# Packed rows kept block behind block and stored eight at a time, a weight fetched as one element, and smaller load slots, in a kernel that reads its input in one pass and writes it scaled in a second

## The chip, the cores and the metric

The kernel runs on one core of one Trainium2 chip. The metric is the device time of one execution in microseconds (us); the time before is the median of three runs. The core has a matrix engine (PE, with its weight loads PEld), a vector engine (DVE), a scalar engine (ACT), GpSimd (POOL) and a sync engine (SP). In this kernel SP does nothing but issue loads, and ACT issues the stores besides its own work. Loads and stores all run on the core's 16 DMA engines.

## The reference

```python
H = W = C = 384                      # x: 1 x H x W x C, bfloat16; w1d: one element
g = jnp.einsum("bhwc->bc", x) / (H * W)
s = jax.nn.sigmoid(g * w1d[0])       # the window k is 1, so nothing is padded
return x * s[:, None, None, :]
```

Each of the 384 channels is averaged over all 147,456 positions. The average, times one weight and through a sigmoid, scales that channel. No output can be written before all of the input has been read, and the input (113.25 MB) is larger than the memory on the core.

## The kernel before

The positions are cut into 1152 "rows". A row of the kernel is one position for each of the 128 partitions, 384 bf16 values each: 768 bytes per partition, 98,304 bytes together. All rows pass through one tile, `arena`, of 275 rows; a range of rows in it is reused for one chunk of the input after another.

**First pass.** SP issues loads in program order. PE sums every row that lands (`sum_rows`, L215 to L239): a matmul with a matrix of ones adds the row into the accumulator `acc`, 1152 matmuls in all. A load into rows that are in use waits until PE has summed what was there. What can stay on the core isn't read again in the second pass:

- 18 rows are copied by ACT into the accumulator memory's seven other banks (`c_ps`, L316);
- 95 rows stay as they are in the parts A (47 rows), Y, U and T (16 each);
- 240 rows are folded. `QS = [16, 16, 16, 12]` gives four groups. In a group with `q`, three times `q` rows `w` stay in one of four areas, and the bits of `q` further rows `u` are hidden in their exponents. `fold` (L272) does that in 15 pieces of 4 `u` rows and 12 `w` rows, with T and Y as scratch rows, and ACT sums a check word for each piece into `seen` (L290), which says later whether any value was out of range.

The other 799 rows (`N_STREAM`) are read in the first pass for their sums alone, and once more in the second pass. The order of loads is written out by hand: `SLOTS` cuts A into load slots, `BEFORE[g]` lists what is streamed ahead of the rows `w` of group `g`, `BETWEEN[g]` what comes between its `w` and its `u`, and `AFTER` what comes behind the last group. At the end come the rows that stay in A, Y and U, and T in parts of 8, 4, 2, 1 and 1 rows (L364).

**The turn.** ACT forms the scale `s_bf` with a sigmoid from `acc` and `w_sc` (L370). `w_sc` is the weight over the number of positions, on all 128 partitions.

**Second pass.** DVE multiplies rows by `s_bf` in place (`scale`, L375), ACT issues their store (`store`, L385), and SP reloads the freed rows with the next of the 799. `unfold` (L393) restores a folded piece, scales it, and stores its 12 `w` rows (L424) and its 4 `u` rows. `from_psum` does the 18 rows of the banks. The order on DVE, ACT and SP comes from a small planner that runs while the program is built (L507 to L619). It keeps two modelled DMA queues, and at each step picks either the next landed rows to scale or, when over `IDLE` = 22 us of DMA work is queued, the next piece to unfold.

`Flow` (L21) turns all this into semaphore waits: each step names the rows that it reads and writes, and the waits follow from that. An area `w` is free for loads once all its pieces are stored.

Of the kernel before, what the change touches and what calls it, by code (L numbers as in the profile page):

```python
# [128 lines left out]
def kernel(  # L129
# [43 lines left out]
    w_bf = pool.tile([P, 1], bf16, name="w_bf")  # L173
# [51 lines left out]
    def sum_rows(a, n):  # L225
# [3 lines left out]
        for i in range(a, a + n):  # L229
            first, last = summed[0] == 0, summed[0] == RPP - 1  # L230
            fl.add(
                "PE", lambda i=i, f=first, l=last: emit(i, f, l),
                reads=[("a", i), "ones"], writes=["acc"],
            )
            summed[0] += 1

# [3 lines left out]

    def dve(fn, out, in_, reads, writes, **kw):
        fl.add("DVE", lambda: getattr(nc.vector, fn)(out=out, **in_, **kw), reads=reads, writes=writes)
# [22 lines left out]
    def three(a, p):  # L265
        return arena[:, a : a + 3 * p, :].rearrange("p (j q) c -> p j q c", j=3).bitcast(u16)

# [4 lines left out]
    def fold(k):  # L272
        g, lo, p = pieces[k]
        w, wc = area(g, lo, p)
        wall = wc[0] + wc[1] + wc[2]
        ua, ta, ya = RAW["U"][0] + lo, RAW["T"][0], RAW["Y"][0]
# [8 lines left out]
        join(w, w, three(ta, p), XOR, wall + rows(ta, 3 * p), wall)  # L285
        join(w[:, 2], w[:, 2], flat(ta + 3 * p, p), XOR, wc[2] + rows(ta + 3 * p, p), wc[2])
# [8 lines left out]
    fl.add("ACT", lambda: nc.scalar.dma_start(out=w_bf[:], in_=w1d.to_broadcast((P, 1))), writes=["w_bf"], dma=True)  # L295
    fl.add("DVE", lambda: nc.vector.memset(ones[:], 1.0), writes=["ones"])  # L296
    fl.add(
        "DVE",
        lambda: nc.vector.tensor_scalar_mul(out=w_sc[:], in0=w_bf[:], scalar1=1.0 / float(HW)),  # L299
        reads=["w_bf"], writes=["w_sc"],  # L300
# [8 lines left out]
    A, Y, U, T = (RAW[n][0] for n in "AYUT")  # L309
# [11 lines left out]
    def stream_all(where, n=None):  # L321
# [9 lines left out]
    SLOTS = [(A, 16), (A + 16, 16), (A + 32, 15)]  # L331
    BEFORE = [
        None,
        areas[2:4] + [(A, 12)],
# [3 lines left out]
    BETWEEN = [[], [], [(A, 13)], [(A, 16)]]  # L338
# [25 lines left out]
    for lo, hi in ((0, 8), (8, 12), (12, 14), (14, 15), (15, 16)):  # L364
# [6 lines left out]
        reads=["acc", "w_sc"], writes=["s_bf"],  # L371
# [21 lines left out]
    def unfold(k, half):  # L393

        g, lo, p = pieces[k]
        q = QS[g]
        w, wc = area(g, lo, p)
        wall = wc[0] + wc[1] + wc[2]
        ra, ba, ca = T + half * PIECE, T + 2 * PIECE, T + 3 * PIECE
        u, b, c = flat(ra, p), flat(ba, p), flat(ca, p)  # L400
        uc, bc, cc = rows(ra, p), rows(ba, p), rows(ca, p)
        bits(u, w[:, 0], SHR, 4, AND, 0x0780, wc[0], uc)
        bits(b, w[:, 1], SHR, 8, AND, 0x0078, wc[1], bc)
        bits(c, w[:, 2], SHR, 12, AND, 0x0007, wc[2], cc)
        join(u, u, b, OR, uc + bc, uc)
        bits(b, w[:, 2], SHL, 4, AND, 0x8000, wc[2], bc)
        join(u, u, c, OR, uc + cc, uc)
        bits(w, w, AND, 0x87FF, OR, 0x3800, wall, wall)
        join(u, u, b, OR, uc + bc, uc)
        wv = w.bitcast(bf16)  # L410
        fl.add(
            "DVE",
            lambda: nc.vector.tensor_tensor(  # L413
                out=wv, in0=wv, in1=s_bf[:, None, None, :].to_broadcast([P, 3, p, C]), op=Op.mult
            ),
# [237 lines left out]
```

## Time and profile before

| | us |
|---|---|
| median of 3 runs | 737.12 (735.68 to 737.66) |
| the profiled execution, its own time | 736.57 |
| its span, first to last instruction | 734.8 |
| DVE busy | 450.7 |
| PE busy | 208.1 |
| ACT busy | 86.7 |

The memory outside the core is read for 191.79 MB and written for 113.25 MB, at 415 GB/s over the span. The profile's page gives busy times in 40 slices of the span, the waits, and the instructions grouped by line and by shape. A line such as L247 is that of a helper (`bits`), so the shape tells which call it was: 128x1536 is four rows of 384, 128x4608 is twelve. A "window" view gives for each stretch of time the busy time of each engine, the clock granted to PE, the busy share of the 16 DMA engines, and the bytes they moved as GB/s. A DMA row with the suffix q is the issue by that engine's queue, not the transfer.

### The profile page before, as it was taken

To read this page: it belongs to the slowest core of one execution; us is meant where nothing else is said; L and a number is where in the kernel's file an instruction comes from. 1 tells how busy PE (TensorE), PEld (TensorE's weight loads), DVE (VectorE), ACT (ScalarE), POOL (GpSimd) and SP (SyncE) were. 2 spreads that over 40 slices of the span, in tenths; PEclk is the share of its full clock that TensorE was granted. 3 is DMA by queue.
4 is the path that set the end of the run, shared out by engine and by line. 5 is a ranking of instruction groups with operands and counts; after the bars stand their busy time and mean duration, and the time that the engine had idled before them with its cause. 6 is when DMAs were issued, how large, how long until landed. Compare 5 with 4: busy or idle time off the path is not lost.

```text
span 734.8 us, 3038 instructions
## 1 busy us (share of the span) xinstructions
PE 208.1 (28%) x1153; PEld 115.9 (16%) x1153; DVE 450.7 (61%) x399; ACT 86.7 (12%) x39; POOL 0.2 (0%) x4
## 2 busy tenths in 40 slices
PE   2877896968687770000000000000000000000000
PEld 1443453535344330000000000000000000000000
DVE  0000002969697709799997579969099999194600
ACT  2000000747475600000000000000000000000000
POOL 0000000000000000000000000000000000000000
PEclk9799998999899995555555555555555555555555
DMA  8999999999999979999999999999999999999996
GB/s 351 426 436 436 427 437 418 442 416 435 417 412 414 387 319 338 431 408 428 428 426 431 427 427 426 440 421 428 421 427 428 439 433 409 426 444 408 425 431 292
DMA packets 29775, 305.25 MB, mean 415 GB/s; under 512 B 3008, under 2 KB 3776, under 8 KB 12992
## 3 DMA queue, kind: packets, MB, share of 16 engines
q1 hardware_dynamic: 12096, 191.80, 61.9%
q10 hardware_dynamic: 17664, 113.25, 36.7%
q8 instruction: 9, 0.15, 0.1%
q14 instruction: 6, 0.05, 0.0%
HBM read 191.79 MB, written 113.25 MB: 415 GB/s over the span
## 4 chain that ended last, share of the span: by engine, by line
DMA 44%; DVE 37%; ACT 7%; PE 4%; ACTq 1%; issue 0%; SPq 0%; DVEq 0%
DMA arena<-in_x_dram 25%; DVE arena L379 19%; DMA out_dram<-arena 19%; DVE arena L247 10%; ACT arena L290 7%; DVE arena L253 4%; PE bank L227 4%; DVE arena L413 4%; ACTq L389 1%; SPq L221 0%; DVEq L106 0%; ACT s_bf L370 0%; PE bank L472 0%; DVE odd L467 0%; DVE odd_i L476 0%
## 5 line engine op out<-in xcount | busy, mean ns | idle before, releaser
L247 DVE TENSOR_SCALAR arena<-arena 128x1536 uint16<-128x1536 uint16 (+1 forms) x210 | 123.8, 639 | 192.3 <-DMA arena<-in_x_dram 126.1
L227 PE MATMUL bank<-arena,ones 128*128 128x384 bf16 x1152 | 207.9, 344 | 66.7 <-DMA arena<-in_x_dram 66.5
L379 DVE TENSOR_TENSOR arena<-arena,s_bf 128x6144 bf16<-128x6144 bf16 (+7 forms) x79 | 198.0, 2567 | 32.6 <-ACT s_bf L370 22.2
L227 PEld LDWEIGHTS bank<-arena,ones 128*128 128x128 bf16 x1152 | 115.8, 102 | 158.4 <-DMA arena<-in_x_dram 68.1
L290 ACT ACTIVATE arena<-arena 128x6144 uint16<-128x6144 uint16 x15 | 79.9, 5324 | 161.8 <-DVE arena L247 161.8
L253 DVE TENSOR_TENSOR arena<-arena 128x1536 uint16<-128x1536 uint16 (+1 forms) x75 | 95.3, 1270 | 1.7 <-PE bank L227 1.1
L413 DVE TENSOR_TENSOR arena<-arena,s_bf 128x4608 bf16<-128x4608 bf16 x15 | 38.3, 2550 | 0.0
L472 PE MATMUL bank<-odd,ones 128*128 128x1 bf16 x1 | 0.2, 186 | 39.7 <-DVE odd L467 39.7
L299 DVE TENSOR_SCALAR w_sc<-w_bf 128x1 f32<-128x1 bf16 x1 | 0.2, 154 | 13.4 <-DMA w_bf<-in_w1d_dram 13.4
L472 PEld LDWEIGHTS bank<-odd,ones 128*128 128x128 bf16 x1 | 0.1, 104 | 40.1 <-DVE odd L467 40.1
L451 DVE TENSOR_TENSOR arena<-bank,s_bf 128x768 bf16<-128x768 bf16 (+2 forms) x15 | 5.0, 390 | 0.1
L316 ACT COPY bank<-arena 128x512 uint32<-128x512 uint32 (+1 forms) x7 | 3.6, 565 | 6.4 <-DMA arena<-in_x_dram 6.4
L370 ACT ACTIVATE s_bf<-bank,w_sc 128x384 bf16<-128x384 f32 x1 | 0.6, 582 | 19.6 <-PE bank L227 19.6
L290 ACT ACTIVATION_READ_ACCUMULATOR arena<-arena 128x1 f32 x15 | 2.8, 186 | 0.0
L621 ACT ACT_TABLE_LOAD x1 | 1.3, 1283 | 0.7 <-PEq L637 0.7
L296 DVE MEMSET ones<- 128x128 bf16 x1 | 0.2, 165 | 1.0 <-SPq L106 1.0
L476 DVE CAST odd_i<-bank 128x1 int32<-128x1 f32 x1 | 0.2, 159 | 0.3 <-PE bank L472 0.3
L467 DVE TENSOR_SCALAR odd<-worst 128x1 bf16<-128x1 f32 x1 | 0.2, 156 | 0.0
L462 DVE TENSOR_REDUCE worst<-seen 128x1 f32<-128x15 f32 x1 | 0.2, 161 | 0.0
L637 POOL MEMSET const-uint8-127<- 128x1 uint8 x1 | 0.1, 102 | 0.0
L637 POOL MEMSET const-bfloat16-1.0<- 128x1 bf16 x1 | 0.1, 101 | 0.0
L637 POOL MEMSET const-float32-0.0<- 128x1 f32 x1 | 0.1, 98 | 0.2 <-issue 0.2
(1 smaller groups left out, 0.1 us busy)
## 6 DMA issues: line engine op xcount, KB each, us to landing
arena<-in_x_dram SPq DMA_DIRECT2D x17, 4608.0 KB, 29.1
out_dram<-arena ACTq DMA_DIRECT2D x46, 1536.0 KB, 30.2
arena<-in_x_dram SPq DMA_DIRECT2D x38, 1536.0 KB, 11.6
arena<-in_x_dram SPq DMA_DIRECT2D x6, 3456.0 KB, 25.6
out_dram<-arena ACTq DMA_DIRECT2D x15, 1152.0 KB, 27.4
arena<-in_x_dram SPq DMA_DIRECT2D x11, 1440.0 KB, 9.8
out_dram<-arena ACTq DMA_DIRECT2D x6, 1440.0 KB, 27.3
out_dram<-arena ACTq DMA_DIRECT2D x16, 384.0 KB, 26.9
```

The lines of the kernel that those rows point to most:

```text
L227: return nc.tensor.matmul(acc, lhsT=ones[:], rhs=arena[:, i, :], start=first, stop=last)
L247: lambda: nc.vector.tensor_scalar(out=dst, in0=src, scalar1=s0, scalar2=s1, op0=op0, op1=op1),
L253: "DVE", lambda: nc.vector.tensor_tensor(out=dst, in0=a, in1=b, op=op), reads=reads, writes=writes
L290: lambda: nc.scalar.activation(out=y, in_=y, func=ACTF.Copy, accum_out=seen[:, k : k + 1]),
L316: lambda bk=bk, lo=lo, hi=hi: nc.scalar.copy(bk[:, 0 : hi - lo].bitcast(u32), psflat[:, lo:hi].bitcast(u32)),
L370: lambda: nc.scalar.activation(out=s_bf[:], in_=acc, func=ACTF.Sigmoid, scale=w_sc[:, 0:1]),
L379: lambda: nc.vector.tensor_tensor(out=v, in0=v, in1=s_bf[:, None, :].to_broadcast([P, n, C]), op=Op.mult),
L389: lambda: nc.scalar.dma_start(out=view(of, r0, n)[:, lo:hi, :], in_=arena[:, a : a + hi - lo, :]),
L413: lambda: nc.vector.tensor_tensor(out=wv, in0=wv, in1=s_bf[:, None, None, :].to_broadcast([P, 3, p, C]), op=Op.mult),
L451: lambda sv=sv, dv=dv, by=by: nc.vector.tensor_tensor(out=dv, in0=sv, in1=by, op=Op.mult),
L472: lambda: nc.tensor.matmul(votes, lhsT=ones[:], rhs=odd[:], start=True, stop=True),
L621: nc.scalar.preload_act_table(ACTF.Sigmoid)
```

## The change

- **Folded areas.** Where an area held all first `w` rows of a group, then all second and all third, it now holds piece behind piece: the 12 `w` rows of a piece are consecutive. `fold` and `unfold` address them as one block, and three DVE instructions of `fold` become one.
- **Stores of unfolded rows.** They are issued for two pieces at a time: 24 consecutive `w` rows and 8 `u` rows (12 and 4 for the odd piece of the last group). The `u` rows are restored in the two halves of T, and the scratch rows for that move from T to Y. Unfolding therefore starts once the rows that stayed in T, Y and U are stored and the banks have been scaled; the banks go to the rows behind `Y + 8`, and these 24 rows become one load slot.
- **The weight.** `w_bf` is one element on one partition instead of 128 copies. A matmul with ones spreads it over the partitions into a column of `bank0`, from which `w_sc` is formed. It stands first on PE.
- **Slots.** A is cut into slots of 12, 12, 12 and 11 rows in the first pass instead of 16, 16 and 15. The second pass cuts it as before (`AGAIN`).
- **Zeros.** 24 and 22 matmuls of a zero matrix are added into `acc` ahead of the rows `w` of the third and the fourth group.
- **Parts.** T comes in 8, 5 and 3 rows at the end of the first pass. The first 16 rows scaled are cut 5, 5, 6 instead of 1, 1, 2, 4, 8.
- **Merged stores.** Where the planner sees over 12 us of DMA work queued, rows of one chunk that are scaled one behind the other are stored together, up to 48.

The diff, cut to what matters (lines that only rename are left out):

```diff
-    w_bf = pool.tile([P, 1], bf16, name="w_bf")
+    w_bf = pool.tile([1, 1], bf16, name="w_bf")
+    zeros = pool.tile([P, P], bf16, name="zeros")
...
+    def keep_warm(n):
+        for _ in range(n):
+            fl.add(
+                "PE",
+                lambda: nc.tensor.matmul(
+                    acc, lhsT=zeros[:], rhs=ones[:, None, :].to_broadcast([P, C // P, P]), start=False, stop=False
+                ),
+                reads=["zeros", "ones"], writes=["bank0"],
+            )
...
     def area(g, lo, p):
-        a, n = areas[g]
-        v = arena[:, a : a + n, :].rearrange("p (j q) c -> p j q c", j=3)[:, :, lo : lo + p, :]
-        q = n // 3
-        return v.bitcast(u16), [rows(a + j * q + lo, p) for j in range(3)]
+        a = areas[g][0] + 3 * lo
+        return a, flat(a, 3 * p), [rows(a + j * p, p) for j in range(3)]
...
-        for j in range(3):
-            bits(flat(ya + j * p, p), w[:, j], AND, 0x7800, XOR, 0x3800, wc[j], rows(ya + j * p, p))
+        bits(flat(ya, 3 * p), w, AND, 0x7800, XOR, 0x3800, wall, rows(ya, 3 * p))
...
-    fl.add("ACT", lambda: nc.scalar.dma_start(out=w_bf[:], in_=w1d.to_broadcast((P, 1))), writes=["w_bf"], dma=True)
+    fl.add("ACT", lambda: nc.scalar.dma_start(out=w_bf[:], in_=w1d.to_broadcast((1, 1))), writes=["w_bf"], dma=True)
...
+        lambda: nc.tensor.matmul(votes, lhsT=ones[0:1, :], rhs=w_bf[0:1, 0:1], start=True, stop=True),
+        reads=["ones", "w_bf"], writes=["bank0"],
...
-    SLOTS = [(A, 16), (A + 16, 16), (A + 32, 15)]
+    SLOTS = [(A, 12), (A + 12, 12), (A + 24, 12), (A + 36, 11)]
+    AGAIN = [(A, 16), (A + 16, 16), (A + 32, 15)]
...
-    BETWEEN = [[], [], [(A, 13)], [(A, 16)]]
+    WARM = [0, 0, 24, 22]
+    BETWEEN = [[], [], SLOTS[:1], SLOTS[:1]]
...
+        keep_warm(WARM[g])
         take(c_w[g], areas[g][0])
...
-    for lo, hi in ((0, 8), (8, 12), (12, 14), (14, 15), (15, 16)):
+    for lo, hi in ((0, 8), (8, 13), (13, 16)):
         take_part("T", lo, hi)
...
-    def unfold(k, half):
+    def unfold(k, at):
...
-        ra, ba, ca = T + half * PIECE, T + 2 * PIECE, T + 3 * PIECE
+        ba, ca = Y, Y + PIECE
...
-        written.append(fl.add(
-            "ACT",
-            lambda: nc.scalar.dma_start(
-                out=view(of, r0, n).rearrange("p (j q) c -> p j q c", j=3)[:, :, lo : lo + p, :], in_=wv
-            ),
-            reads=wall, dma=True,
-        ))
-        written.append(store(c_u[g], ra, lo, lo + p))
+    def store_unfolded(g, lo, n, at):
+        written.append(store(c_w[g], areas[g][0] + 3 * lo, 3 * lo, 3 * (lo + n)))
+        written.append(store(c_u[g], at, lo, lo + n))
...
-            can = unfolded < len(pieces) and halves[unfolded % 2] and now > 6
-            if not psum_done and extra == {"Y": 0, "U": 0}:
-                from_psum(Y)
+            can = kk < len(pieces) and not held["T"] and not held["YU"] and from_banks
+            if can and pieces[kk][1] % PAIR == 0:
+                can = half[pair % 2]
+            if not from_banks and not held["YU"] and not held["T"]:
+                from_psum(Y + 2 * PIECE)
...
+                if then or ahead < MERGE:
+                    store(chunk, a + since, since, hi)
+                    stored_to = None
+                else:
+                    stored_to = since
```

The planner's new order shows best in the instructions themselves. First, SP's loads at the end of the first pass, from the 36 streamed rows ahead of the last group's `w` (128x13824) to the last of the rows that stay in A (128x5760 or 128x4224); 128x6144 is 16 rows, 128x4608 is 12. Before:

```order
L221 DMA arena<-in_x_dram 128x13824
L221 DMA arena<-in_x_dram 128x6144 [waits f_PE]
L221 DMA arena<-in_x_dram 128x6144
L221 DMA arena<-in_x_dram 128x5760
L221 DMA arena<-in_x_dram 128x13824 [waits f_PE]
L221 DMA arena<-in_x_dram 128x6144 [waits f_PE]
L221 DMA arena<-in_x_dram 128x4608 [waits f_DVE]
L221 DMA arena<-in_x_dram 128x6144 [waits f_PE]
L221 DMA arena<-in_x_dram 128x5760 [waits f_PE]
L221 DMA arena<-in_x_dram 128x6144 [waits f_PE] x2
L221 DMA arena<-in_x_dram 128x5760 [waits f_PE]
```

And now:

```order
L222 DMA arena<-in_x_dram 128x13824
L222 DMA arena<-in_x_dram 128x4608 [waits f_PE]
L222 DMA arena<-in_x_dram 128x4608 x2
L222 DMA arena<-in_x_dram 128x4224
L222 DMA arena<-in_x_dram 128x13824 [waits f_PE]
L222 DMA arena<-in_x_dram 128x4608 [waits f_PE]
L222 DMA arena<-in_x_dram 128x4608 [waits f_DVE]
L222 DMA arena<-in_x_dram 128x4608 [waits f_PE] x2
L222 DMA arena<-in_x_dram 128x4224 [waits f_PE]
L222 DMA arena<-in_x_dram 128x4608 [waits f_PE] x3
L222 DMA arena<-in_x_dram 128x4224 [waits f_PE]
```

Between the last `w` (the second 128x13824) and the last `u` (the load that waits for DVE) stood 16 rows and stand 12; behind `u` the slots that PE must have summed come in fours of 12, 12, 12 and 11 rows.

Second, DVE behind the scale of the first 95 rows, where `L253` joins and `L247` shifts belong to an unfolding and `L451` is the banks (their first two of 15 instructions are shown). Before:

```order
L379 TENSOR_TENSOR arena<-arena,s_bf 128x6144 x3
L247 TENSOR_SCALAR arena<-arena 128x1536 x3
L253 TENSOR_TENSOR arena<-arena 128x1536
...
L379 TENSOR_TENSOR arena<-arena,s_bf 128x6144
L451 TENSOR_TENSOR arena<-bank_71,s_bf 128x768
L451 TENSOR_TENSOR arena<-bank_71,s_bf 128x256
```

And now (`L394` scales, `L454` is the banks, `L256` the first shift of an unfolding):

```order
L394 TENSOR_TENSOR arena<-arena,s_bf 128x6144 [waits f_SP2]
L394 TENSOR_TENSOR arena<-arena,s_bf 128x6144 [waits f_SP3]
L394 TENSOR_TENSOR arena<-arena,s_bf 128x5760 [waits f_SP4]
L454 TENSOR_TENSOR arena<-bank_72,s_bf 128x768 [waits f_ACT10]
L454 TENSOR_TENSOR arena<-bank_72,s_bf 128x256
...
L256 TENSOR_SCALAR arena<-arena 128x1536 [waits f_ACT8]
```

One unfolding stood ahead of the banks; now all three reloaded slots of A are scaled there, then the banks, and the first unfolding comes behind them.

Third, the stores that ACT issues at that place. Before, with 12 `w` rows written as 384 runs of 1536 elements:

```order
L424 DMA out_dram<-arena 384x1x1536 [waits f_DVE]
L389 DMA out_dram<-arena 128x1536 [waits f_DVE]
L389 DMA out_dram<-arena 128x6144 [waits f_DVE]
L389 DMA out_dram<-arena 128x6912 [waits f_DVE]
```

And now, with 24 `w` rows (128x9216) and 8 `u` rows (128x3072) behind the banks' 18 (128x6912):

```order
L404 DMA out_dram<-arena 128x6912 [waits f_DVE]
L404 DMA out_dram<-arena 128x6144 [waits f_DVE]
L404 DMA out_dram<-arena 128x9216 [waits f_DVE]
L404 DMA out_dram<-arena 128x3072 [waits f_DVE]
```

The runs of an unfolded store grow from 4 rows to 24 (`w`) and 8 (`u`) per partition.

More of the change, by code (lines that the diff above doesn't have):

```diff
@@ L526, with nothing, release, backlog @@
-    waiting = deque()
-    busy_area = {g: sum(1 for p in pieces if p[0] == g) for g in range(len(QS))}
-    halves = [True, True]
-    extra = {"Y": 1, "U": 1}
-    def release(name):
+    PENDING, MERGE = 22.0, 12.0
+    now = dve_at = 0.0
+    loads, stores, waiting = deque(), deque(), deque()
+    landed, free = deque(), deque()
+    todo = 0
+    def nothing():
+        pass
+    def release(a, n):
+        return lambda: free.append((a, n))
+    def backlog():
+        return sum(e[1] for q in (loads, stores) for e in q) + ROW * sum(e[1] for e in waiting)
@@ L552 @@
     stall = 0.0
[L553 removed]
     while True:
         if dve_at <= now:
[L558 to L566 removed]
+            kk = at_piece
@@ L586 @@
+                if not asked:
                     verdict()
-                    verdict_done = True
+                    asked = True
         while waiting and waiting[0][0] <= now:
             _, n, then = waiting.popleft()
-            queue(stores, n, then)
-        if unfolded == len(pieces) and not checked and all(v == 0 for v in busy_area.values()) and all(halves):
+            stores.append([now + LAT, n * ROW, then])
+        if at_piece == len(pieces) and not checked and not any(left.values()) and all(half):
```

185 lines of the change are left out of this document (84 added, 101 removed).

## The prediction

> **What bounds the kernel now.** I read the page first: its slices and its DMA queues.
>
> ```profile
> GB/s 351 426 436 436 427 437 418 442 416 435 417 412 414 387 319 338 431 408 428 428 426 431 427 427 426 440 421 428 421 427 428 439 433 409 426 444 408 425 431 292
> ...
> q1 hardware_dynamic: 12096, 191.80, 61.9%
> q10 hardware_dynamic: 17664, 113.25, 36.7%
> ```
>
> Loads (q1) and stores (q10) together keep the 16 DMA engines busy for 98.6% of the span. So the kernel is a stream of 305 MB, and only two things can shorten it: time in which the engines have nothing to move, and packets that move slowly. I then cut the span into stages with the windows view; the last two columns are the DMA engines' busy share and GB/s.
>
> ```profile
> 0.00:6.00 6.00, 0.00 (x0) 0.00 (x0) 0.17 (x1) 1.28 (x1) 0.20 (x4) 1.00 0.66 223
> 6.00:13.00 7.00, 4.52 (x17) 2.24 (x18) 0.00 (x0) 3.59 (x7) 0.00 (x0) 1.00 1.00 398
> 20.00:200.00 180.00, 143.55 (x791) 80.56 (x792) 61.84 (x88) 43.34 (x16) 0.00 (x0) 0.91 1.00 430
> 200.00:204.00 4.00, 4.00 (x25) 2.20 (x23) 3.97 (x4) 3.77 (x1) 0.00 (x0) 1.00 0.87 317
> 232.00:258.00 26.00, 20.27 (x121) 11.23 (x119) 20.61 (x28) 16.25 (x6) 0.00 (x0) 1.00 0.98 390
> 268.00:276.00 8.00, 5.55 (x32) 2.97 (x32) 0.81 (x3) 0.58 (x1) 0.00 (x0) 1.00 0.41 157
> 276.00:290.00 14.00, 0.00 (x0) 0.00 (x0) 14.00 (x10) 0.00 (x0) 0.00 (x0) 0.59 0.91 329
> 290.00:728.00 438.00, 0.19 (x1) 0.10 (x1) 326.48 (x236) 0.00 (x0) 0.00 (x0) 0.50 1.01 426
> 728.00:734.80 6.80, 0.00 (x0) 0.00 (x0) 0.00 (x0) 0.00 (x0) 0.00 (x0) 0.50 0.16 65
> ```
>
> The long stretch 20 to 200 us shows what an undisturbed stream does: 430 GB/s. I count each stage's loss against that, its length times (1 - rate/430). The start loses 2.9 and 0.5 us, the hole at 200 us 1.05, the end of the first pass 2.4 (232 to 258), the turn 5.1 and 3.3, the second pass 4.1 over 438 us, the end 5.8. These losses come to 25 us; the rest of the span is the stream itself. DVE is busy for 326 of the 438 us of the second pass, so it has 112 us to spare there.
>
> **The change part by part.** The sum is made against the profiled execution's own 736.57 us, which is 0.55 us below the median of 737.12.
>
> *Stores of unfolded rows.* 240 rows (15 pieces of 16), 23.6 MB, leave today in runs of four rows, 3072 bytes. Two stretches hold stores alone: at 530.8 us those of unfolded pieces, at 537 us those of 16 rows.
>
> ```profile
> 530.80:535.20 4.40, 0.00 (x0) 0.00 (x0) 1.66 (x4) 0.00 (x0) 0.00 (x0) 0.50 1.02 413
> 537.00:549.00 12.00, 0.00 (x0) 0.00 (x0) 11.93 (x13) 0.00 (x0) 0.00 (x0) 0.50 1.01 430
> ```
>
> The engines are busy in both, but the short runs go at 413. 23.6 MB take 57.1 us at 413 and 54.9 at 430, so 2.2 us. The `u` rows only go up to runs of eight, which no stretch shows alone; at worst they stay at 413, and the `w` rows' three quarters give 1.7. I take -2.0; zero is the other bound, if a stream mixed with loads (most of the second pass) hides it.
>
> *The two holes of the first pass.* SP waits for PE there:
>
> ```profile
> SPq L221 <- PE bank L227: 59.7, 11, 15.3
> ...
> 201.44 0.80 SPq L221 DMA_DIRECT2D arena<-in_x_dram  x2
> ...
> 234.39 0.33 SPq L221 DMA_DIRECT2D arena<-in_x_dram  x1
> ...
> 189.69 14.32 PE L227 MATMUL bank<-arena,ones 128*128 128x384 bf16 x77 [8.12 <-DMA arena<-in_x_dram]
> 224.36 16.98 PE L227 MATMUL bank<-arena,ones 128*128 128x384 bf16 x95 [5.60 <-DMA arena<-in_x_dram]
> 242.65 2.77 PE L227 MATMUL bank<-arena,ones 128*128 128x384 bf16 x16 [1.31 <-DMA arena<-in_x_dram]
> ```
>
> The first row is SP's waits from 196 to 260 us. PE goes in program order, so a slot that is summed behind a long load `w` comes free only after all of `w` has landed and been summed. `w` of the third group lands at 189.7 us; PE sums its 48 rows and the 13 of the slot behind, and SP may reload the slot at 201.44. The loads queued ahead have run dry by then: the hole at 200 us. At a steady 173 ns a row (2.77 over 16) 77 rows need 13.3 us and took 14.32, so PE lost 1.0 us to a slow start after 8.12 us of idleness; 95 rows lost 0.5 after 5.60.
>
> Now 48 + 12 rows stand there instead of 48 + 13 (0.2 us), and the zeros may save the slow start. In the second place it is 36 + 12 instead of 36 + 16: four rows less and 0.5 us of slow start put the issue of 234.39 some 1.2 us earlier, while the rows queued behind it stay the same (12 + 12 + 35 for 16 + 12 + 31). Behind that the slots go round in fours: a slot's way from issue to reissue holds four rows less to load (4 x 0.229 us at 430 GB/s) and to sum (4 x 0.173), 1.6 us in all, while a round still moves 47 rows. That slack is what the round lacked. I take -0.6 of the 1.05 and -1.9 of the 2.4, together -2.5; the bounds are zero and -3.4.
>
> Whether the zeros help hangs on PE's clock. Two sums of the first stretch show it:
>
> ```profile
> 62.33 9.49 PE L227 MATMUL bank<-arena,ones 128*128 128x384 bf16 x47 [3.69 <-DMA arena<-in_x_dram]
> 73.24 7.97 PE L227 MATMUL bank<-arena,ones 128*128 128x384 bf16 x48 [1.43 <-DMA arena<-in_x_dram]
> ```
>
> After 1.43 us of idleness 48 rows take 7.97 us; after 3.69 us 47 take 9.49. The 24 zeros take 4.2 us at 173 ns and stand right behind the earlier sums, so 3.9 us of the 8.12 stay idle, and PE may start slowly all the same. The 22 zeros (3.8 us) leave 1.8 of 5.60, which is short enough. So I count half of the first gain and all of the second. The Trainium skill (TensorE: Matmul & The Clock Gate, HAM oscillation) says that PE is throttled again by idle gaps over about 3.4 us. By that rule alone the first place would keep its slow start and the sum would be 0.3 us smaller; the two rows above agree with it.
>
> *The start.* The weight today is 128 elements to 128 partitions, which trickle in:
>
> ```profile
> w_bf<-in_w1d_dram ACTq DMA_DIRECT2D x1, 0.2 KB, 13.7
> ```
>
> It takes 13.7 us to land, and just in that time (6 to 13 us) the loads run at 398. One element can give back at most those 0.5 us; I take -0.4, with zero as the bound, since the first large loads also start there. The sum of the first rows now waits for the weight on PE. Should it land as late as today, PE starts on the first 18 rows some 14 us into the span. The first load that waits for these sums has 180 rows queued ahead of it (three loads of 48 rows and one of 36), 41 us of transfer. So this costs nothing.
>
> *The turn.* The first store leaves once the first rows are scaled:
>
> ```profile
> L379 DVE TENSOR_TENSOR arena<-arena,s_bf 128x1920 bf16<-128x1920 bf16 x1 | 1.2, 1152 | 0.0
> L379 DVE TENSOR_TENSOR arena<-arena,s_bf 128x384 bf16<-128x384 bf16 x2 | 0.6, 354 | 22.2 <-ACT s_bf L370 22.2
> ...
> 275.58 0.84 ACTq L389 DMA_DIRECT2D out_dram<-arena  x2
> ```
>
> Five rows take 1152 ns and one row 354, so the first issue moves from 275.58 by 0.8 us. Against that, the 16 rows need three instructions instead of five, and stores of one row at a time do not fill the engines (329 GB/s up to 290 us). I take +0.2, between -0.6 and +0.8. The last rows of T cost nothing: PE sums all 16 behind the last load in any case.
>
> *The order of the second pass.* Today one unfolding stands ahead of the banks and hides a wait for stores.
>
> ```profile
> DVE arena L247 <- DMA out_dram<-arena: 64.3, 7, 20.4
> ...
> 304.09 1.03 DVE L247 TENSOR_SCALAR arena<-arena 128x1536 uint16<-128x1536 uint16 x2 [4.84 <-DMA out_dram<-arena]
> ...
> 314.53 3.35 DVE L379 TENSOR_TENSOR arena<-arena,s_bf 128x6144 bf16<-128x6144 bf16 x1
> ```
>
> It fills 304.1 to 314.5, 10.4 us. Now it comes behind the banks, which wait until U's store has landed, and stores leave by pairs, so DVE may do 20 us of unfolding without giving a store. The cover is the queued DMA work, which the planner keeps at 22 us before it starts a piece. I take +0.4 for small gaps, between 0 and 10.
>
> *At nothing.* The chain of waits shows the last `u` land (first row) and the last check of its fold:
>
> ```profile
> 215.13 15.65 DMA arena<-in_x_dram
> ...
> 249.58 5.42 ACT arena L290 x2
> ```
>
> The fold takes 24.2 us, 230.8 to 255.0, and a load into Y waits for it. Behind the last `u` 129 rows are queued ahead of that load, 29.5 us, so 5 us cover `fold`'s one wide shift, whose time no row shows alone. Without cover it could cost what three short ones take. Nothing either for the second memset, for merged stores (16-row stores already run at 430, as the 48-row loads of 20 to 200 us do), and for the end, where 9 rows instead of 5 are last. The end's 5.8 us are mostly one or two DMA engines that finish late; that may move by 2 us either way.
>
> Sum: -2.0 - 2.5 - 0.4 + 0.2 + 0.4 = -4.3, and 736.57 - 4.3 = **732.3 us**.
>
> **The rivals.**
>
> *DMA starves early in the second pass (slower).* While DVE waits for U's store it has nothing to unfold, and later gives no store for two pieces. If the queues run empty, the 10.4 us of the displaced unfolding show up in full: 732.3 + 10 = 742. For it: DVE already waits 64.3 us for stores, and T and Y are now locked to each other. Against it: DVE has 112 us to spare, and the rate of 426 shows no gap today. It decides the matter if less than some 10 us of DMA work is queued when the first unfolding begins.
>
> *The holes stay.* If the loads are held up less by PE than by the landing of the long `w`, 2.5 us come back: 734.8, no change by the measure below. For it: SP's issues at 201.44 and 234.39 follow the start of the sums of `w` by 11.8 and 10.0 us, and the change takes only about one of these away. Against it: the rounds behind 234 us have no `w` in them.
>
> *Short runs cost nothing in a mixed stream.* Then 2.0 us come back: 734.3. For it: the whole second pass, with loads beside the stores, loses only 4.1 us.
>
> *The late engines catch up.* Longer runs may spread the work more evenly, and the end's 5.8 us fall by 3: 729.3. For it: 65 GB/s over 6.8 us is work for few engines; against it: nothing in the change aims there.
>
> **How the numbers follow.** A measurement of this kernel can tell about 0.3% (2.2 us) from no change, so faster means under 734.9 and slower over 739.3. The forecast has 0.52 (0.50 of it faster), the late engines 0.14 (faster), the mixed stream 0.10 and the holes 0.14 (each on the border: 0.05 faster in each case, the rest no change), the starvation 0.10 (slower). That is 0.74 faster, 0.16 the same, 0.10 slower. The range reaches from the late engines with the holes, the start and the turn at their better bounds (0.9, 0.1 and 0.8 us), 727.5, to the holes and the stores without gain, 736.8. The starvation is left out.
>
> **What would show it.** After: 426 to 430 GB/s through 200 to 260 us; 430 where stores of unfolded rows are alone; a few us less of DMA share in q10; PE's sums behind the fourth group's `w` at 173 ns from the first. I am wrong if a hole appears between 300 and 350 us, if the first store is issued no earlier than 275.6 us, or if the end behind the last full stretch grows beyond 7 us.

## The result, and the profile after

| | us |
|---|---|
| before, median of 4 runs | 736.40 (735.00 to 737.66) |
| after, median of 4 runs | 736.59 (734.73 to 737.46) |
| ratio | 1.0, 95% interval 0.9971 to 1.0028 |
| after, profiled execution: own time, span | 734.73, 732.9 |

The time did not change. It lies 0.2 us inside the upper end of the range (736.8), but the forecast was a gain of 4.3 us, and none can be measured. That it lies inside is luck: 736.8 stood for holes and stores without gain, and it was another term that took the gain away. The profiled execution is the shortest of the four, so its stages show 1.9 us less than before although the median shows none.

The slices and the queues of the page after:

```profile
GB/s 382 421 443 420 439 429 435 422 422 432 420 412 405 397 309 356 429 430 433 426 433 440 418 432 433 439 426 427 427 445 426 427 420 426 430 431 423 422 435 236
...
q1 hardware_dynamic: 11952, 191.80, 61.8%
q10 hardware_dynamic: 8930, 113.25, 36.3%
```

The stores go out in half as many packets (8930 for 17664), and the last slice fell from 292 to 236 GB/s. The windows of after; the last two columns are again the DMA engines' busy share and GB/s:

```profile
6.00:13.00 7.00, 4.75 (x18) 2.28 (x18) 0.00 (x0) 3.59 (x7) 0.00 (x0) 1.00 1.08 467
20.00:200.00 180.00, 147.74 (x820) 83.34 (x819) 62.02 (x71) 44.57 (x17) 0.00 (x0) 0.91 1.00 430
196.00:268.00 72.00, 60.73 (x352) 33.61 (x350) 48.94 (x55) 37.92 (x14) 0.00 (x0) 0.98 0.99 407
268.00:276.00 8.00, 5.38 (x32) 3.05 (x32) 1.97 (x2) 0.58 (x1) 0.00 (x0) 1.00 0.26 102
276.00:290.00 14.00, 0.00 (x0) 0.00 (x0) 14.00 (x9) 0.00 (x0) 0.00 (x0) 0.58 0.97 369
290.00:660.00 370.00, 0.19 (x1) 0.10 (x1) 304.89 (x234) 0.00 (x0) 0.00 (x0) 0.50 1.01 430
660.00:700.00 40.00, 0.00 (x0) 0.00 (x0) 13.26 (x4) 0.00 (x0) 0.00 (x0) 0.50 0.99 420
700.00:720.00 20.00, 0.00 (x0) 0.00 (x0) 1.96 (x1) 0.00 (x0) 0.00 (x0) 0.50 1.02 437
720.00:728.00 8.00, 0.00 (x0) 0.00 (x0) 0.00 (x0) 0.00 (x0) 0.00 (x0) 0.50 0.56 238
728.00:732.90 4.90, 0.00 (x0) 0.00 (x0) 0.00 (x0) 0.00 (x0) 0.00 (x0) 0.50 0.05 20
```

And of before, where the stretch is not among the prediction's rows:

```profile
196.00:268.00 72.00, 57.92 (x338) 32.40 (x335) 50.87 (x70) 37.91 (x14) 0.00 (x0) 0.98 0.99 407
290.00:660.00 370.00, 0.19 (x1) 0.10 (x1) 303.56 (x229) 0.00 (x0) 0.00 (x0) 0.50 1.01 426
660.00:700.00 40.00, 0.00 (x0) 0.00 (x0) 22.92 (x8) 0.00 (x0) 0.00 (x0) 0.50 1.01 425
700.00:720.00 20.00, 0.00 (x0) 0.00 (x0) 0.00 (x0) 0.00 (x0) 0.00 (x0) 0.50 1.01 429
720.00:728.00 8.00, 0.00 (x0) 0.00 (x0) 0.00 (x0) 0.00 (x0) 0.00 (x0) 0.50 1.00 425
```

Counted as in the prediction (length times 1 minus rate/430), the losses are:

| stretch | before | after |
|---|---|---|
| 6 to 13 us, start | 0.5 | -0.6 |
| 196 to 268, both holes | 3.85 | 3.85 |
| 268 to 290, turn | 8.4 | 8.1 |
| 290 to 660 | 3.4 | 0.0 |
| 660 to the end | 6.4 | 8.8 |

(Over 370 us, one GB/s is 0.9 us. The window view counts a packet where it starts, so a short stretch can show more than the engines move in it: from 6 to 13 us their busy share is 1.08.) So the second pass does run at 430 up to 660 us, as forecast, and the start is better. The holes lost as much as in the one profile of before, and the end lost 2.4 us more. At the end the engines do not run out together: between 720 and 728 us they are busy for 0.56 of the time, where before it was 1.00. The last store's 16 landings, one for each DMA engine, lie 6.5 us apart in the trace, before 4.15: some engines had fallen behind, and by the end they had not caught up.

The first pass after, from the timelines of PE and SP:

```profile
180.72 4.06 PE L243 MATMUL bank<-ones,zeros 128*128 128x384 bf16 x24
188.57 14.21 PE L228 MATMUL bank<-arena,ones 128*128 128x384 bf16 x76 [3.79 <-DMA arena<-in_x_dram]
217.83 3.74 PE L243 MATMUL bank<-ones,zeros 128*128 128x384 bf16 x22
224.26 16.04 PE L228 MATMUL bank<-arena,ones 128*128 128x384 bf16 x89 [2.69 <-DMA arena<-in_x_dram]
...
200.21 39.64 SPq L222 DMA_DIRECT2D arena<-in_x_dram  x13
```

PE stood idle only 3.79 us ahead of the third group's `w`, and still took 14.21 us for 76 rows (13.1 at 173 ns). SP issued 11.6 us after the start of the sums, where it was 11.8: the slot comes free hardly sooner after that.

The turn and DVE's waits in the second pass:

```profile
273.42 0.58 ACT L385 ACTIVATE s_bf<-bank,w_sc 128x384 bf16<-128x384 f32 x1 [19.83 <-PE bank L228]
...
L394 DVE TENSOR_TENSOR arena<-arena,s_bf 128x1920 bf16<-128x1920 bf16 x2 | 2.2, 1155 | 22.4 <-ACT s_bf L385 22.4
275.22 6.01 ACTq L404 DMA_DIRECT2D out_dram<-arena  x5
...
DVE arena L394 <- DMA arena<-in_x_dram: 72.8, 12, 17.0
DVE arena L256 <- DMA out_dram<-arena: 18.1, 2, 10.3
```

And the scale of before:

```profile
274.58 0.58 ACT L370 ACTIVATE s_bf<-bank,w_sc 128x384 bf16<-128x384 f32 x1 [19.58 <-PE bank L227]
```

The first store left at 275.22, before at 275.58; the scale is formed 1.16 us sooner, so from there to the first store it takes 1.80 us where it took 1.00. DVE waits 18.1 us for stores where it was 64.3 (for loads 72.8 where it was 9.9), and no hole follows: the rate up to 660 us is 430.

### The profile page after: what moved, and what is told of

Read it like the earlier page. It is cut to its first block, busy times and chain, and to the rows that moved or that the text cites. A ratio compares the mean times of both kernels' runs of the same rounds, so it can differ in the third digit from the quotient of the medians.

```text
span 732.9 us, 3059 instructions
## 1 busy us (share of the span) xinstructions
PE 216.1 (29%) x1200; PEld 120.5 (16%) x1200; DVE 443.4 (60%) x371; ACT 86.7 (12%) x39; POOL 0.2 (0%) x4
## 3 DMA queue, kind: packets, MB, share of 16 engines
q10 hardware_dynamic: 8930, 113.25, 36.3%
## 4 chain that ended last, share of the span: by engine, by line
DMA 46%; DVE 28%; another core or an unknown queue 9%; ACT 8%; PE 3%; issue 0%; SPq 0%
DMA arena<-in_x_dram 29%; DMA out_dram<-arena 17%; DVE arena L394 15%; DVE arena L256 9%; ACT arena L296 8%; DVE arena L262 4%; PE bank L228 3%; SPq L222 0%; ACT s_bf L385 0%; SPq L658 0%; SPq L106 0%
## 5 line engine op out<-in xcount | busy, mean ns | idle before, releaser
L394 DVE TENSOR_TENSOR arena<-arena,s_bf 128x6144 bf16<-128x6144 bf16 (+7 forms) x95 | 237.2, 2541 | 95.9 <-DMA arena<-in_x_dram 72.8
L256 DVE TENSOR_SCALAR arena<-arena 128x1536 uint16<-128x1536 uint16 x180 | 115.9, 688 | 160.2 <-DMA arena<-in_x_dram 139.9
L243 PE MATMUL bank<-ones,zeros 128*128 128x384 bf16 x46 | 7.8, 326 | 0.0
L454 DVE TENSOR_TENSOR arena<-bank,s_bf 128x768 bf16<-128x768 bf16 (+2 forms) x15 | 5.0, 390 | 0.1
L243 PEld LDWEIGHTS bank<-ones,zeros 128*128 128x128 bf16 x46 | 4.5, 98 | 3.0
```

The lines of the kernel that those rows point to most:

```text
L243: lambda: nc.tensor.matmul(acc, lhsT=zeros[:], rhs=ones[:, None, :].to_broadcast([P, C // P, P]), start=False, stop=False),
L256: lambda: nc.vector.tensor_scalar(out=dst, in0=src, scalar1=s0, scalar2=s1, op0=op0, op1=op1),
L394: lambda: nc.vector.tensor_tensor(out=v, in0=v, in1=s_bf[:, None, :].to_broadcast([P, n, C]), op=Op.mult),
L454: lambda sv=sv, dv=dv, by=by: nc.vector.tensor_tensor(out=dv, in0=sv, in1=by, op=Op.mult),
```

## The experiments

Ratios are against runs of the kernel before on the same chip, with 95% intervals; the kernel before took 736.7 to 738.3 us in these comparisons.

**1 and 2. The changed kernel again, and without merged stores.** The second differs in one line:

```diff
-                if then or ahead < MERGE:
+                if True:
```

> The changed kernel once more, for a second profile and more times. Theory A (the late engines): the start, the turn and the second pass keep their gains (about 1.1, 0.3 and 2.6 us against the profile of the kernel before) and the end loses 7 to 8 us again, since some DMA engines finish up to 6.5 us behind the first; time within 0.3% of the kernel before. Theory B (chance): the end's loss differs by more than 2 us from the first profile, and the first profile's end is no property of the kernel.

> The changed kernel without merged stores: every run of rows is stored once it is scaled, 16 rows at most. Theory A, with the merged stores as the cause: their 36,864-byte packets run slow late in the second pass and put single engines behind, so here the end loses 5 to 6 us as in the kernel before, the rest keeps its gains, and the time is 1.5 to 2.5 us below the changed kernel's. Rival: merging is not the cause; the end loses 7 to 8 us and the time stays within 1 us.

Changed kernel again: 736.61 (731.65 to 740.36, 12 runs), 0.9983 (0.9964 to 1.0002). Without merging: **732.25** (731.28 to 732.95, 6 runs), 0.9937 (0.9918 to 0.9955). The windows of the first, then of the second (its span is 730.1):

```profile
660.00:700.00 40.00, 0.00 (x0) 0.00 (x0) 13.18 (x5) 0.00 (x0) 0.00 (x0) 0.50 1.00 413
700.00:720.00 20.00, 0.00 (x0) 0.00 (x0) 6.39 (x3) 0.00 (x0) 0.00 (x0) 0.50 1.04 445
720.00:728.00 8.00, 0.00 (x0) 0.00 (x0) 0.00 (x0) 0.00 (x0) 0.00 (x0) 0.50 0.59 251
728.00:735.00 7.00, 0.00 (x0) 0.00 (x0) 0.00 (x0) 0.00 (x0) 0.00 (x0) 0.50 0.05 20
```

```profile
660.00:700.00 40.00, 0.00 (x0) 0.00 (x0) 11.77 (x4) 0.00 (x0) 0.00 (x0) 0.50 1.00 428
700.00:720.00 20.00, 0.00 (x0) 0.00 (x0) 0.00 (x0) 0.00 (x0) 0.00 (x0) 0.50 1.01 430
720.00:728.00 8.00, 0.00 (x0) 0.00 (x0) 0.00 (x0) 0.00 (x0) 0.00 (x0) 0.50 0.52 220
728.00:735.00 7.00, 0.00 (x0) 0.00 (x0) 0.00 (x0) 0.00 (x0) 0.00 (x0) 0.70 0.00 1
```

Merging costs 4.4 us (3.4 by the two ratios). It takes back what the rest of the change brings, and the time varies over 8.7 us in 12 runs instead of 1.7 in 6 (the kernel before: 6.0 in 29). From 660 us to the end the first loses 10.9 us (the changed kernel's first profile 8.8) and the second 6.2. So the loss at the end comes back, more than theory A gave for it, and its size differs by 2 us from one execution to the next. In the first profile the engines are fully busy from 660 to 700 us and yet move 413 GB/s; the spread of the last landings is 9.1 us, without merging 4.5. In the second pass of experiment 1 the packets of 48-row transfers (36,864 bytes) take 1364 ns as a rule, but 1% of them over 1.8 (loads) or 1.9 us (stores).

**3. The changed kernel without the zeros.**

```diff
-    WARM = [0, 0, 24, 22]
+    WARM = [0, 0, 0, 0]
```

> The changed kernel without the 24 and 22 matmuls of zeros. Theory: they hide nothing, since PE idles 3.8 and 2.7 us behind them and starts slowly all the same; the loads behind the long rows w are issued at the same times within 0.3 us, the two holes stay as they are, and the time is the same within 1 us. Rival (the clock): without them the first slot behind w comes free 0.5 to 1 us later in both places, the holes lose 1 to 2 us more, and the time rises by as much.

738.39 us (735.89 to 740.13, 12 runs), 1.0017 (1.0 to 1.0035): 1.8 us over experiment 1, the two intervals just touching. So the zeros seem to help, as the rival says, but not at both places. The first reload leaves at 199.74 us, no later than in the changed kernel (200.21). Behind the fourth group's `w` PE takes 85 rows in 16.30 us (192 ns a row) after 6.25 us of idleness, where experiment 1 took 84 in 13.82 (165) after 2.64.

**4. The kernel before with the weight as one element.**

```diff
-    w_bf = pool.tile([P, 1], bf16, name="w_bf")
+    w_bf = pool.tile([1, 1], bf16, name="w_bf")
...
+        lambda: nc.tensor.matmul(votes, lhsT=ones[0:1, :], rhs=w_bf[0:1, 0:1], start=True, stop=True),
```

> The kernel before with one edit: the weight comes as one element and is spread by a matmul. Theory: the 128 two-byte descriptors cost the first loads 1.1 us between 6 and 14 us; that stretch goes from 372 to 433 GB/s here and all later stages move up by 1.1 us, so the time falls by about 1 us (0.15%). Rival: it is the second load's start that slows that stretch, which stays below 390 GB/s, and the time doesn't move.

736.41 us (733.84 to 739.51, 12 runs), 0.9985 (0.9969 to 1.0002).

```profile
6.00:13.00 7.00, 4.98 (x16) 2.34 (x17) 0.00 (x0) 3.59 (x7) 0.00 (x0) 1.00 1.09 469
```

The row says 469 from 6 to 13 us where it said 398, which is 1.2 us. With the bytes of each packet spread over the time that it took, the trace gives 433 where it gave 364, which is 1.1. The time agrees (-1.1), though its interval just includes nothing.

**5. Second-pass loads of at most 16 rows, and no merging.** Each 16 rows are a chunk of their own here, so that they are also stored and come free alone.

```diff
             n = min(n, N_STREAM - todo)
+            if n > 16:
+                free.appendleft((a + 16, n - 16))
+                n = 16
```

> The changed kernel without merged stores, and with the loads of the second pass cut to 16 rows at most, so that no packet there is over 12,288 bytes (the two-piece stores of 18,432 bytes stay). Theory (long packets of loads and stores side by side run slow and set single engines back): the 4.5 us between the first and the last engine at the end fall below 2 us, and the time falls by 2 us below the 732.2 of the kernel without merged stores, to 0.991 of the kernel before. Rival: 48-row loads do no harm; the spread stays at 4 to 5 us and the time within 1 us.

730.38 us (729.77 to 731.95, 4 runs), 0.9898 (0.9883 to 0.9912).

```profile
660.00:700.00 40.00, 0.00 (x0) 0.00 (x0) 12.03 (x4) 0.00 (x0) 0.00 (x0) 0.50 1.01 430
720.00:728.00 8.00, 0.00 (x0) 0.00 (x0) 0.00 (x0) 0.00 (x0) 0.00 (x0) 0.50 0.71 301
728.00:735.00 7.00, 0.00 (x0) 0.00 (x0) 0.00 (x0) 0.00 (x0) 0.00 (x0) 0.70 0.00 1
```

From 660 us to the end at 730.1 this loses 4.6 us (before 6.4, after 8.8), and the last landings are 2.0 us apart. No packet of a second-pass load is longer than 12,288 bytes now, and 99% of the packets of that length took at most 460 ns. Slots also come free in smaller pieces here, and no run tells that apart from the shorter packets.

**6. Without merging, slots reloaded in the order in which they come free.** The rows `u` of the last group are summed three slots later, and the hand-written lists begin with the slot that is free first.

> The changed kernel without merged stores, and with the two holes of the first pass attacked by order alone: ahead of the last group's long rows the slots are reloaded in the order in which they were summed (those that are free first), and the sums of the last rows u come behind those of three slots. Theory (PE frees the slots too late behind a long load w): the stretch 196 to 268 us loses under 1 us against 430 GB/s instead of 1.8 to 3.4, so 1 to 2 us less time, 0.991 to 0.992 of the kernel before. Rival (the landing of w itself, not the order, sets it): no change within 0.5 us.

732.04 us (731.03 to 732.7, 6 runs), 0.9924 (0.9912 to 0.9935): no gain over 0.9937. Its profile loses 2.0 us between 196 and 268 (418 GB/s), that of experiment 2 2.2. The order of the slots is not what is left of the holes.

**7. The kernel before with folded pieces block behind block,** each piece's 12 `w` rows stored as one run; nothing else.

```diff
-        a, n = areas[g]
-        v = arena[:, a : a + n, :].rearrange("p (j q) c -> p j q c", j=3)[:, :, lo : lo + p, :]
+        a = areas[g][0] + 3 * lo
+        v = arena[:, a : a + 3 * p, :].rearrange("p (j q) c -> p j q c", j=3)
...
+        written.append(store(c_w[g], areas[g][0] + 3 * lo, 3 * lo, 3 * (lo + p)))
```

> The kernel before with one edit: a folded piece's 12 rows w lie one behind the other and are stored as runs of 12 rows; fold's instructions, the order, the rows u and all else are as before. Theory: three quarters of the 23.6 MB go at 430 instead of 413 GB/s, the second pass loses 1.7 us less, and the time falls by 1 to 2 us (0.997 to 0.9985). Rival: short runs are hidden in the mixed stream; no change.

734.26 us (731.52 to 738.26, 12 runs), 0.9957 (0.9938 to 0.9976): 3.2 us, between 1.8 and 4.6; the best value is above the 1.7 that 413 against 430 gives for these rows. In the trace a packet of 3072 bytes takes 121 ns in the mixed stream too, and one of 9216 takes 347, so 1920 packets for 5760 save 1.9 us on each of 16 engines. The rest of the 3.2 is not explained. The twelve times fall into two groups, seven from 731.5 to 734.4 and five from 736.2 to 738.3. The profile is one of the upper group, and its second pass is hardly faster (427 from 290 to 660 us). The edit also shortens the wide shift of `unfold` (1354 ns for 1751), whose rows are contiguous now, and no run takes that apart from the stores.

**8. The changed kernel, merged stores held back as long but issued in parts of 16 rows.**

```diff
-                    store(chunk, a + since, since, hi)
+                    for e in range(since, hi, 16):
+                        store(chunk, a + e, e, min(e + 16, hi))
```

> The changed kernel with the merged stores held back as long as there, but then issued as parts of 16 rows one behind the other. It tells the packet's size from the time of issue. If the size of the packets (36,864 bytes) makes engines late, this behaves as the kernel without merging: spread at the end 4 to 5 us, time about 732 us (0.994). If the late issue does it (rows held until 48 are scaled), it behaves as the changed kernel: spread 6.5 us or more, time 736 to 737 (0.998 to 1.0).

734.13 us (733.15 to 736.3, 6 runs), 0.996 (0.9944 to 0.9975). By the time it lies between experiments 1 (0.9983) and 2 (0.9937), and the intervals overlap on both sides. By the other sign that was named, the spread of the last landings, it behaves as without merging: 3.9 us, and the last load lands at about 681 us (experiment 2: 4.5 and 680; the changed kernel: 6.5 and 700). The profile is that of its fastest run, though. So the length of the packets has a part in the cost; how large the part of holding back is stays open.

**9. Experiment 5 with zeros that fill nearly the whole wait.**

```diff
-    WARM = [0, 0, 24, 22]
+    WARM = [0, 0, 42, 34]
```

> The kernel with each part stored as it is folded and with second-pass loads of at most 16 rows (730.38, 0.9898 of before), and 42 and 34 products of zeros in place of 24 and 22, so that they nearly fill the waits for the third and fourth w. Theory A (TensorE is slow to start because it stood idle for 2.7 to 3.8 us; what sets the two holes is the time of its first sums): the sums behind w run at about 173 ns from the first, the first slot's reload is issued 1 to 2 us sooner, 196 to 268 us lose about 1 us and not 1.7 to 3.8, and the time falls by 1 us more, to 0.987 to 0.989. Theory B (the shorter idle time changes nothing, the landing of w and the sums at full speed set the reload): within 0.001 of 0.9898.

```profile
180.97 6.99 PE L243 MATMUL bank<-ones,zeros 128*128 128x384 bf16 x42
188.58 12.53 PE L228 MATMUL bank<-arena,ones 128*128 128x384 bf16 x76 [0.62 <-DMA arena<-in_x_dram]
223.99 12.19 PE L228 MATMUL bank<-arena,ones 128*128 128x384 bf16 x74
...
198.53 41.41 SPq L222 DMA_DIRECT2D arena<-in_x_dram  x14
```

730.49 us (729.22 to 730.9, 6 runs), 0.9917 (0.9895 to 0.994). The trace did what theory A says: 76 rows at 165 ns from the first, and the reload at 198.53 instead of 200.21. The time did not follow; a gain of 1 us over experiment 5 is not to be seen, and the interval is too wide to exclude one. In experiment 2, with the 24 zeros, PE also happened to start at once, so the smaller number already serves in some executions.

**10. The kernel before with only the loads of at most 16 rows** (the edit of experiment 5).

> The kernel before with only one edit: loads of the second pass of at most 16 rows a piece. Theory A (the large transfers of loads and stores side by side set single DMA engines back, and the end waits for these): the last store's landings, 4.15 us apart before, come within 2 us, and the time falls by about 2 us, to 0.9965 to 0.998. Theory B (in the kernel before only the 12-row loads' neighbours, the stores in runs of 3072 bytes, cost, and the end is only the last rows' latency): no change, 0.999 to 1.001.

736.07 us (734.89 to 737.89, 12 runs), 0.9999 (0.9984 to 1.0013).

```profile
196.00:268.00 72.00, 58.92 (x334) 32.79 (x333) 50.86 (x70) 37.92 (x14) 0.00 (x0) 0.93 0.96 396
720.00:728.00 8.00, 0.00 (x0) 0.00 (x0) 0.00 (x0) 0.00 (x0) 0.00 (x0) 0.50 1.00 419
728.00:735.00 7.00, 0.00 (x0) 0.00 (x0) 0.00 (x0) 0.00 (x0) 0.00 (x0) 0.50 0.35 142
```

The landings came together as theory A says (1.6 us apart, before 4.15), and 660 us to the end at 734.1 loses 4.3 us for 6.4. But the gain of 2 us did not appear in the time. In this profile the holes ate it (396 GB/s from 196 to 268, before 407). Experiments 4 and 7, with the same slots and no zeros, also have 395 and 396, so the 407 of before is the exception; why the time gains nothing is not known. So the short loads alone are not shown to help the kernel before.

**11. All that helps or may help:** experiments 5, 6 and 9 in one kernel.

> Everything that has helped or may help together: each part stored as it is folded, second-pass loads of at most 16 rows, slots reloaded in the order in which they come free, 42 and 34 products of zeros. Theory A (the holes and the end add up): 0.986 to 0.988, about 728 to 729 us, 196 to 268 us lose under 1 us. Theory B (what is saved in the first pass is lost again at the turn or at the end): 0.989 to 0.991.

**729.89 us** (729.31 to 730.83, 6 runs), 0.9911 (0.9889 to 0.9933). It is about 7 us under the kernel before, and cannot be told from experiments 5 and 9. Theory A's 728 to 729 was not reached.

**12. The changed kernel, merging left, each load issued as transfers of at most 16 rows.**

```diff
-            load(chunk, a)
+            for lo in range(0, n, 16):
+                load(chunk, a + lo, lo, min(n, lo + 16))
```

> The changed kernel with its merged stores of up to 48 rows left as they are; only a load of the second pass is issued as transfers of at most 16 rows one behind another, so that a packet of a load is never longer than 12,288 bytes. The order of the work on VectorE and the moments at which rows come free stay. Theory A (it is the long packets of loads and of stores side by side that set single DMA engines back): the last stores' landings, 6.5 to 9.1 us apart, come within 5 us, and the time falls from 736.6 to 733 to 734.5, 0.995 to 0.997 of before. Theory B (the long stores, held back and sent in one, set the engines back by themselves): the spread stays at 6 us and over and the time at 0.998 to 1.0.

737.9 us (734.43 to 742.34, 12 runs), 0.9994 (0.9974 to 1.0015). Theory A's gain is not there. The last landings are 0.2 us apart, as it would have them, but that bears out neither theory, since the cut opened a new hole:

```profile
660.00:700.00 40.00, 0.00 (x0) 0.00 (x0) 18.10 (x6) 0.00 (x0) 0.00 (x0) 0.50 1.01 422
700.00:720.00 20.00, 0.00 (x0) 0.00 (x0) 8.64 (x3) 0.00 (x0) 0.00 (x0) 0.50 0.62 261
```

The last loads landed at 720.1 us, where in the changed kernel it was 700.6, and a store of 48 rows had to wait for its last part; 20 us at 261 lose 7.9 us. Why the loads came late shows in the queues between 640 and 655 us, with the share of the engines' time last. This kernel:

```profile
q10 hardware_dynamic: 164, 4.09, 65.1%
q1 hardware_dynamic: 180, 2.00, 31.3%
```

And experiment 5, where in this stretch no packet of either side is longer than 12,288 bytes:

```profile
q10 hardware_dynamic: 337, 3.71, 58.0%
q1 hardware_dynamic: 331, 2.69, 42.4%
```

In both, loads and stores get about as many packets. A queue's share of the time thus goes with the length of its packets, and 16-row loads beside stores of 36 and 48 rows get half of what the stores get. The Trainium skill (DMA: Bandwidth & Descriptors, Queues, rings and completion order) says that each DMA engine takes its queues in turn, one packet at a time; the counts agree.

## Why the prediction was right, and where it failed

| term | predicted | shown |
|---|---|---|
| stores of unfolded rows | -2.0 | -3.2 (-4.6 to -1.8) alone |
| two holes | -2.5 | about -2 over the profiles; none in the first |
| start | -0.4 | -1.1 |
| turn | +0.2 | first store 0.8 later after the scale; stage -0.3 in the profile |
| order of the second pass | +0.4 | nothing seen |
| merged stores | at nothing | +4.4 |
| the end | 0, by 2 either way | +2.4 in the profile, part of the merging |

**The step that failed is one word in "At nothing": merged stores.** I costed them by "16-row stores already run at 430, as the 48-row loads of 20 to 200 us do". Both rows are of one direction alone. In the first pass, with loads alone, 99% of the 36,864-byte packets take at most 1375 ns. In the mixed stream 1% of them take over 1.7 to 2.0 us (the two profiles of the changed kernel), on both sides. The 48-row loads do so in the kernel before as well (over 1.9 us), and merging adds as many 48-row packets of stores that do. What the second pass's packets took beyond the median of their length is, shared over 16 engines, 2.1 us before, 2.2 and 4.0 in the two profiles of the changed kernel, 1.8 without merging, and 0.4 in experiment 5. The spread of the last landings goes the same way (4.15; 6.5 and 9.1; 4.5; 2.0). That the engines that end last are those that met the slow packets is argued; the trace does not name a packet's engine. Experiment 2, the change without that one edit, took 732.25 us: the sum of the other terms was near (-4.3 predicted, -4.6 by its ratio). The parts measured alone add up to some 6.5 us, each with an uncertainty of 1 to 1.5 us, so the sum is known better than its terms. I put 0.74 on faster because that one edit had no term and no rival.

**The stores** were the best founded term: the whole second pass from 290 to 660 us went from 426 to 430 GB/s. The other profiles of the changed kernel and its variants have 428 or 429 there. The rival that short runs cost nothing in a mixed stream is out by experiment 7 and by its packets' times. In the changed kernel the same count gives 2.8 us for these rows.

**The holes** came out near the forecast in size, though not in the first profile. With the old slots and no zeros the scale is formed at 274.58, 276.24 and 276.37 us (before, experiments 7 and 10) and at 275.33 with the new start (experiment 4). In the six profiles with the new slots in their first order and 24 and 22 zeros it is formed at 272.0 to 274.1. Less the start's 1.2 us, that is 1.9 us sooner on average. At the first place the forecast that PE may start slowly all the same came true: of seven profiles with 24 zeros, PE started slowly in six (9 or more of its first 30 sums start over 0.25 us apart), and only in experiment 2 it did not. At the second place PE started slowly in all five profiles without zeros. With 22 zeros it did in two of seven: the changed kernel, with 89 rows in 16.04 us (180 ns a row) after 2.69 us of idleness, and experiment 5. So "short enough" held most of the time, although 2.5 to 2.7 us and not 1.8 were left in these two and in experiments 1 and 12. What the shorter slots bring alone is not shown: 404 GB/s from 196 to 268 us without the zeros (experiment 3), where 395 to 407 stood before. The gain comes and goes with the execution. At the first place of experiment 2 PE began at once after 3.61 us:

```profile
188.57 12.52 PE L228 MATMUL bank<-arena,ones 128*128 128x384 bf16 x76 [3.61 <-DMA arena<-in_x_dram]
```

The rule that I weighed (the Trainium skill, TensorE: Matmul & The Clock Gate, HAM oscillation: idle gaps over about 3.4 us throttle PE) is not a sharp limit here: 2.69 us was followed by slow sums and 3.61 was not. The trace of before had shown as much at 84.16 us, where 48 rows take 9.47 us after 2.94 us of idleness. Another section of the same page of the Trainium skill (Part 1: The HAM clock gate) says that the clock's activity window runs freely, so that the number of slow matmuls differs from run to run; the rows after 2.69 and 3.61 us agree with it.

**The start** was mis-sized because I took the view's 398 GB/s as what the engines moved. With the bytes of each packet spread over its time it was 364, so 1.1 us and not 0.5 could come back. The ceiling of some 430 held: the stage reaches 433, and the 467 to 469 of the view come from packets that reach over its edges. The gain was 1.1 us.

**The turn and the order** went as argued: the first store leaves 0.8 us later after the scale, as forecast, and 0.36 us sooner in all only because the scale is formed 1.16 us sooner. The starvation rival (a hole from 300 to 350 us) is out.

**The end** grew by 2.4 us from 660 us on, more than the 2 us that I allowed. An end that "behind the last full stretch grows beyond 7 us" was a sign of being wrong that I had named; by 720 us the engines are no longer all busy, and the loss from there is 8.2 us. The rival "late engines catch up" had the right place and the wrong sign. The engines do come closer together once loads and stores are both short (experiment 5).

**What stays open:** why a long packet is slow now and then; how the cost of merging splits between length and holding back; what splits the times of experiment 7 into two groups; and why the kernel before gains nothing measurable from shorter loads although its end comes together (experiment 10).

## What to carry to other kernels

When the DMA engines are busy from start to end, look at them one by one at the end of the trace: the spread of the last landings can be time (though experiment 10 narrowed it and gained none), and a larger transfer that is no slower by itself can widen it. Keep packets of loads and stores short enough and alike in length (here 16 rows, 12,288 bytes, for both was better than 48), since a queue's share of the engines goes with its packet length. A change in several parts needs each part run alone; here six parts brought 4 to 5 us and a seventh took them away in silence.

## What the runs showed of the hardware that was not expected

- In a stream of mixed loads and stores, packets of 36,864 bytes take 1364 ns, but 1% of them over 1.7 to 2.0 us (the changed kernel's two profiles), stores and loads alike, and also when only the loads are that long (kernel before). With loads alone 99% took at most 1375 ns. Packets of 12,288 bytes took at most 464 ns in 99 of 100 cases (experiment 5). The engines' last landings lie 6.5 to 9.1 us apart with long loads and stores, and 2.0 in experiment 5.
- A weight loaded as 128 two-byte elements slowed the loads beside it from 433 to 364 GB/s for some 7 us.
- The two DMA queues shared the engines packet by packet (164 packets of stores against 180 of loads, 65.1 against 31.3% of the time; 40 of the 344 are four-byte writes).
- PE started slowly after 2.69 us of idleness (180 ns a row over 89 rows) and at full speed after 3.61 (165 ns over 76).
